# Regrouping the rows of a two-filter FFT mix, moving half a fold and most product sums to TensorE, and ordering the work by a list scheduler

## The chip, the cores and the metric

The kernel runs on one core of one Trainium2 chip. The metric is the device time of one execution in microseconds (us). The profiled span, from the first to the last instruction, is 1.5 to 2.1 us shorter than the timed run. Runs that the measurement marks as slow (over 1.5% above the fastest of the same kernel) are left out of the ratios and their intervals; the medians are over all runs, slow ones too.

## The reference, cut to what matters

```python
x = A_x                                                  # 1 x 2048 x 1024, bf16
g = sigmoid((x * gate_w).sum(-1, keepdims=True))         # one gate per row
def filt(x, w_r, w_i):                                   # weights 2048 x 513
    X = rfft2(x.astype(float32), axes=(-2, -1))
    return irfft2(X * (w_r + 1j * w_i), s=(2048, 1024), axes=(-2, -1)).astype(bfloat16)
return g * filt(x, A_w_r, A_w_i) + (1 - g) * filt(x, B_w_r, B_w_i)
```

Both filters use the same x, so the forward transform is done once. The kernel does all transforms as matmuls with constant matrices.

## The kernel before

Rows are split as n = 16 n1 + n2. *Stage 1* transforms over n1 (after "folding" each row: sums and differences of mirrored halves). *Stage d* transforms over the columns. The *forward n2 stage* finishes the row transform. Then each filter gets four products and two sums (*prod*), the *inverse n2 stage* (i1), the inverse column stage (dinv), and one last stage that mixes the two filters by the gate (s1inv). The row transform has 513 columns; the last one, column 512, is carried separately by small matmuls and small products. Every stage ends in a copy of 128x1024 from PSUM (PS in the profile, the memory that the matmuls write) to SBUF (the memory of R, RING and the other tiles that the matmuls read), called an eviction below, by ScalarE (ACT) or VectorE (DVE).

```python
# ... fold: two levels, four VectorE operations
dve(ns, tt(Sx, lo, hi, ALU.add), reads, [skey + ("S",)])
dve(ns, tt(Tx, lo, hi, ALU.subtract), reads, [skey + ("T",)])
for i, op in enumerate((ALU.add, ALU.subtract)):
    dve(ns, tt(o, f, r, op), ...)                        # second level
# ... stage 1: 8 matmuls of N=128 for each of 16 n2
# ... gate_row(c): 8 matmuls, then a one-partition copy; four of them, the last ones right before stage d

def stage_s2(kg):                                        # forward n2 stage, 128x128 weights
    fns = [mm(pslot(s, 0, [[1, 512]]), A, Q(0, 0, 512), True, False),
           mm(pslot(s, 512, [[1, 512]]), Cc, Q(0, 0, 512), True, False),
           mm(pslot(s, 1, [[1, 511]]), Cn, Q(1, 1, 511), False, True),
           mm(misc(6, kg, [[1, 1]]), Cn, Q(1, 0, 1), True, True),
           # ... two more

def prod(b, m):                                          # per filter and pair of groups
    dve(1230, tt(..., x, w, ALU.mult), r, ["t0"])
    dve(1230, tt(..., x, ws, ALU.mult), r, ["t1"])
    for c, op in enumerate((ALU.subtract, ALU.add)):     # the product sums
        dve(680, tt(..., op), [f"t{c}"], [("P", m % 2, c)])

for t in range(16 + 5):                                  # the order: loops written by hand
    if t < 16: stage_d(t)
    if 1 <= t < 17: stage_s2(t - 1)
    if t >= 5: stage_i1(0, t - 5)
    if t >= 2 and t % 2 == 0: prod(t // 18, t // 2 - 1 - t // 18 * 8)
    # ...
```

In these kernels each engine works through its own instructions in the order in which they were emitted, and semaphores hold it where data or a buffer is missing (in the first hand order below VectorE stands 4.8 us behind one eviction with eight folds to do). So the order of emission is the schedule.

Of the kernel before, what the change touches and what calls it, by code (L numbers as in the profile page):

```python
# [11 lines left out]
PW = 128  # L12
# [7 lines left out]

def make_consts():
# [4 lines left out]
    n1 = np.arange(128)[:, None, None]  # L26
    n2 = np.arange(16)[None, :, None]
    kord = (np.arange(16)[:, None] + 16 * np.arange(4)[None, :]).reshape(-1)
    k1 = kord[None, None, :]
    a = pi2 * ((16 * n1 * k1 + n2 * k1) % 2048) / 2048.0  # L30
    F = np.zeros((128, 16, 64, 2))
    F[..., 0] = np.cos(a)
    F[..., 1] = -np.sin(a)
    F[:, :, 0, 1] = (-1.0) ** np.arange(128)[:, None]
    C["F"] = F.reshape(128, 2048)
    R = np.zeros((64, 2, 16, 128))
    at = a.transpose(2, 1, 0)
    R[:, 0] = np.cos(at) / 2048
    R[:, 1] = np.sin(at) / 2048
    R[0, 1] = ((-1.0) ** np.arange(128))[None, :] / 2048  # L40
    C["RM"] = R.reshape(128, 2048)

    m = np.arange(256)[None, :]
    DM = np.zeros((128, 4, 2, 256))
    for h in range(2):
        d = (h * 128 + np.arange(128))[:, None] + 0.5
        lev, lod = 2 * m, 2 * m + 1
        les = np.where(m == 0, 512, 2 * m)
        DM[:, 0, h] = np.cos(pi2 * lev * d / 1024)
        DM[:, 1, h] = -np.sin(pi2 * lod * d / 1024)  # L50
        DM[:, 2, h] = -np.sin(pi2 * les * d / 1024)
        DM[:, 3, h] = np.cos(pi2 * lod * d / 1024)
# [11 lines left out]

    S2 = np.zeros((2, 3, 128, 128))
    KI = np.zeros((2, 2, 128, 2, 16, 4, 2))
    for z in range(2):
        for pm in range(2):
            for k2 in range(16):
                for ii in range(4):  # L70
                    i = ii if pm == 0 else 3 - ii
                    po = k2 * 8 + pm * 4 + ii
                    spec = (z == 1 and i == 0)
                    for q2 in range(16):
                        w = np.exp(-1j * pi2 * q2 * (k2 + (1 if (pm == 1 and not spec) else 0)) / 16)
                        if spec and pm == 1:
                            w = w * np.exp(-1j * pi2 * q2 * 64 / 2048)
                        r0, r1 = q2 * 8 + i * 2, q2 * 8 + i * 2 + 1
                        wr, wi = w.real, w.imag
                        if spec:  # L80
                            r = r0 if pm == 0 else r1
                            S2[z, 0, r, po] = wr
                            S2[z, 1, r, po] = wi
                        else:
                            sg = 1.0 if pm == 0 else -1.0
                            S2[z, 0, r0, po] = wr
                            S2[z, 0, r1, po] = -sg * wi
                            S2[z, 1, r0, po] = wi
                            S2[z, 1, r1, po] = sg * wr
                        cr, ci = wr, -wi  # L90
                        K = KI[z, :, po, :, q2, i, :]
                        if spec:
                            ri = pm
                            K[0, 0, ri], K[1, 0, ri] = cr, -ci
                            K[0, 1, ri], K[1, 1, ri] = ci, cr
                        else:
                            K[0, 0, 0], K[1, 0, 0] = cr, -ci
                            K[0, 0, 1], K[1, 0, 1] = -sg * ci, -sg * cr
                            K[0, 1, 0], K[1, 1, 0] = ci, cr
                            K[0, 1, 1], K[1, 1, 1] = sg * cr, -sg * ci  # L100
        S2[z, 2] = -S2[z, 1]
    C["S2"] = S2.transpose(2, 0, 1, 3).reshape(128, 768)
    C["KI"] = KI.reshape(2, 2, 128, 256).transpose(2, 0, 1, 3).reshape(128, 1024)
    gs = np.full((64, 2), 8.0)
    gs[:, 1] = -8.0
    gs[0] = 4.0
    C["GS"] = np.repeat(gs.reshape(128, 1), 16, axis=1)
    one = np.zeros((128, 2))
    one[0] = 1.0
    C["ONE"] = one  # L110
    idt = np.zeros((128, 16))
    idt[:16] = np.eye(16)
    C["ID"] = idt
# [3 lines left out]
class Op:  # L117
    __slots__ = ("eng", "idx", "fns", "deps", "raw", "dma", "clock", "need", "count", "waits", "pos")

    def __init__(self, eng, idx, fns, dma, pos):  # L120
        self.eng, self.idx, self.fns, self.dma, self.pos = eng, idx, fns, dma, pos
        self.deps, self.raw = set(), set()
        self.need = False
        self.count = 0


class Sched:
# [9 lines left out]
    def op(self, eng, fns, reads=(), writes=(), dma=False):  # L137
        if not isinstance(fns, (list, tuple)):
            fns = [fns]
# [3 lines left out]
        for k in reads:  # L143
            assert k in self.writer, k
            o.deps |= self.writer[k]
            o.raw |= self.writer[k]
        for k in writes:
            o.deps |= self.writer.get(k, set())
            o.deps |= self.readers.get(k, set())
# [84 lines left out]

def bass_gated_mix__spectral_gfnet__spectral_gfnet__prompt_kernel(
    nc, A_x, A_w_r, A_w_i, B_x, B_w_r, B_w_i, gate_w, out
):
    C = make_consts()
# [16 lines left out]
    FM = sb("FM", 2048)  # L255
    DM = sb("DM", 2048)
    S2 = sb("S2", 768)
    KI = sb("KI", 1024)
    DI = sb("DI", 2048)
    RM = sb("RM", 2048)  # L260
    GS = sb("GS", 16)
    ONE = sb("ONE", 2)
    ID = sb("ID", 16)
    V6 = sb("V6", 256)
    RING = sb("RING", 11264)
    GROW = sb("GROW", 512)
# [3 lines left out]
    ZG = sb("ZG", 16)  # L270
    G8 = sb("G8", 8)
# [8 lines left out]
    WR = {0: R5, 1: R2}  # L280


    load = {"act": 0.0, "dve": 0.0}
    slot_n = [0]
    nslots = [3]

    def slot():
        s = slot_n[0] % nslots[0]
        slot_n[0] += 1
        return s  # L290

    def dve(ns, fns, reads, writes):
        load["dve"] += ns
        return S.op("dve", fns, reads, writes)

    def ev(n, outap, inap, reads, writes, eng=None, bias=0.0):
        ca, cd = 170 + 0.833 * n, 150 + 1.04 * n
        if eng is None:
            eng = "act" if load["act"] + ca <= load["dve"] + cd + bias else "dve"
        load[eng] += ca if eng == "act" else cd  # L300
        if eng == "act":
            S.op("act", lambda e: e.activation(outap, inap, ACT.Copy), reads, writes)  # L302
        else:
            S.op("dve", lambda e: e.tensor_copy(outap, inap), reads, writes)  # L304

    def pslot(s, off, dims, p0=0, np_=128):
        return ap(PS, s * 1024 + off, dims, p0, np_)

    def misc(b, off, dims, np_=128):
        return ap(PS, b * 512 + off, dims, 0, np_)  # L310
# [7 lines left out]
    def dma(eng, pairs, reads, writes, kind=True):  # L318
        S.op(eng, [lambda e, d=d, s=s: e.dma_start(d, s) for d, s in pairs], reads, writes, dma=kind)  # L319

    def cload(eng, t, key, n):
        dma(eng, [(ap(t, 0, [[1, n]]).bitcast(dt.uint16), cst[key].ap())], [], [key])


    def xload(a, b):
        dma("sp", [(ap(R1, a * 1024, [[1024, b - a], [1, 1024]]), xv[:, a:b, :])], [], [("x", i) for i in range(a, b)])

    xload(0, 2)
    cload("sp", FM, "F", 2048)
    dma("act", [(ap(R2, 2048, [[1, 1024]], 0, 1), gate_w.rearrange("(o d) -> o d", o=1))], [], ["gw"])  # L330
    cload("act", ONE, "ONE", 2)
    for a, b in ((2, 4), (4, 8), (8, 12), (12, 16)):
        xload(a, b)
    cload("sp", DM, "DM", 2048)
    cload("sp", S2, "S2", 768)
    cload("sp", KI, "KI", 1024)
    cload("sp", GS, "GS", 16)
    cload("sp", ID, "ID", 16)

    def wload(b):  # L340

        prs = []
        T = WR[b]
        P = pit[id(T)]
        for ii in range(4):
            for c in range(2):
                for pm in range(2):
                    src = wsrc[b][c]
                    n = src.shape[-1]

                    def part(r0, step, k0, k1):
                        prs.append((AP(T, (4 * pm + ii) * P + (2 * k0 + c) * NS, [[8 * P, 16], [2 * NS, k1 - k0], [1, n]]),
                                    AP(src.tensor, src.offset + r0 * n, [[128 * n, 16], [step * n, k1 - k0], [1, n]])))
                    if pm == 0:
                        part(16 * ii, 1, 0, 16)
                    elif ii < 3:
                        part(80 + 16 * ii, -1, 0, 16)
                    else:
                        part(127, -1, 1, 16)
                        part(64, 1, 0, 1)  # L360
        dma("sp", prs, [], [("W", b)] + (["zrow", "gwt"] if b else []))
    wload(0)


    def fold(n, src, soff, tmp, st, dst, doff, p0, np_, ns, reads, skey, writes):
# [280 lines left out]
```

## Time and profile before

| | before |
|---|---|
| time, median of 2 runs | 158.36 us |
| profiled span | 155.9 us |
| busy TensorE / VectorE / ScalarE | 124.6 / 120.4 / 121.6 us |
| stage 1 ends (first matmul with DM, that of stage d) | 34.2 us |

The first lines come from the page of the kernel before: part 1 (busy time and share of the span) and part 4 (the chain of waits that ended last, by engine). PE is TensorE's matmuls, PEld its weight loads, POOL GpSimd, SPq the queue of SyncE that issues transfers; "issue" is time for which the profile shows no wait.

```profile
PE 124.6 (80%) x1015; PEld 89.8 (58%) x1024; DVE 120.4 (77%) x193; ACT 121.6 (78%) x132; POOL 0.2 (0%) x4
...
ACT 39%; PE 27%; DVE 21%; issue 6%; DMA 4%; SPq 1%; DVEq 0%
```

No engine is over 80% busy, and the chain changes hands among three engines. What is missing is found at the borders of stages. The next lines are from the timeline of the kernel before, 26 to 36 us. The columns are start, length, engine, line, operation, output <- inputs, shape and count; in brackets stands how long the engine was idle before and who ended that.

```profile
26.29 1.29 DVE L316 TENSOR_TENSOR R<-RING 128x1024 bf16<-128x1024 bf16 x2
...
28.63 1.89 PE L313 MATMUL PS<-R,G 128*1 128x512 bf16 x8
30.56 0.59 ACT L302 ACTIVATE R<-PS 1x512 bf16<-1x512 f32 x1 [0.33 <-PE PS L313]
31.20 1.89 PE L313 MATMUL PS<-R,G 128*1 128x512 bf16 x8 [0.68 <-ACT R L302]
33.12 0.59 ACT L302 ACTIVATE R<-PS 1x512 bf16<-1x512 f32 x1 [1.98 <-PE PS L313]
33.76 0.55 PE L313 MATMUL PS<-ONE,R 1*128 1x1 bf16 x16 [0.68 <-ACT R L302]
34.24 1.92 PE L313 MATMUL PS<-DM,R 128*128 128x256 bf16 x16
34.35 0.17 DVE L316 TENSOR_TENSOR ZG<-PS,GS 128x16 bf16<-128x16 f32 x1 [6.77 <-PE PS L313]
```

VectorE's folds end at 27.6 us. Then TensorE and ScalarE do the last two gate rows by turns, one partition at a time, while VectorE is idle for 6.77 us; only then does stage d start. The groups of VectorE by shape, part of the same profile, hold the operations that the change moves (busy us, mean ns | idle before):

```profile
L316 DVE TENSOR_TENSOR RING<-R 128x2048 bf16<-128x2048 bf16 x32 | 37.7, 1219 | 8.4 <-ACT R L302 8.4
L316 DVE TENSOR_TENSOR RING<-RING 128x512 bf16<-128x512 bf16 x64 | 24.0, 421 | 2.2 <-ACT RING L302 1.4
L316 DVE TENSOR_TENSOR RING<-RING 128x1024 bf16<-128x1024 bf16 x32 | 20.6, 684 | 0.3 <-PE PS L313 0.3
L316 DVE TENSOR_TENSOR R<-RING 128x1024 bf16<-128x1024 bf16 x16 | 10.3, 688 | 0.3
L316 DVE TENSOR_TENSOR RING<-R 128x1024 bf16<-128x1024 bf16 x16 | 10.3, 684 | 5.7 <-DMA R<-in_A_x_dram 5.7
```

From the top: 32 products, 64 final butterflies, 32 product sums, and the two levels of the fold. Their sum is 102.9 us.

### The profile page before, as it was taken

The page shows a single profiled execution, that of the slowest core. Times are in us where ns is not written, and L with a number is a line of the kernel's source. Part 1 is how long each engine was busy: PE and PEld are TensorE (multiplying, and loading weights), DVE is VectorE, ACT ScalarE, POOL GpSimd, SP SyncE. Part 2 cuts the span into 40 slices and gives each one's busy share as a digit, 9 for nine tenths or more (in the row PEclk, how much of TensorE's full clock was granted, in tenths as well). Part 3 has the DMA queues.
Part 4 walks back from the last instruction along what each step waited for, and adds up shares of the span by engine and source line. Part 5 has one row for each costly group of instructions (what it writes and reads, how often), then busy time and mean ns, then how long its engine had stood idle before and what let it go on. Part 6 is the DMA issues. An engine that isn't in the chain of part 4 may idle for free.

```text
span 155.9 us, 2541 instructions
## 1 busy us (share of the span) xinstructions
PE 124.6 (80%) x1015; PEld 89.8 (58%) x1024; DVE 120.4 (77%) x193; ACT 121.6 (78%) x132; POOL 0.2 (0%) x4
## 2 busy tenths in 40 slices
PE   0155887788989999999836999969999899898920
PEld 0144654345656777776524888857777666565600
DVE  0689999000489988998999999979725688999992
ACT  3045789819999899799954799999997699888850
POOL 0000000000000000000000000000000000000000
PEclk9999999999999999999985799999999999999995
DMA  4899999999999960000000000000000033343333
GB/s 148 307 427 421 293 208 212 219 233 242 252 249 254 247 199 0 0 0 4 0 0 0 1 4 0 0 0 4 0 0 1 4 135 135 128 147 135 135 135 135
DMA packets 13165, 19.53 MB, mean 125 GB/s; under 512 B 1505, under 2 KB 9825, under 8 KB 12770
## 3 DMA queue, kind: packets, MB, share of 16 engines
q1 hardware_dynamic: 13008, 19.37, 45.1%
q8 instruction: 8, 0.13, 0.4%
q10 hardware_dynamic: 146, 0.00, 0.1%
q14 instruction: 3, 0.02, 0.0%
HBM read 15.17 MB, written 4.19 MB: 124 GB/s over the span
## 4 chain that ended last, share of the span: by engine, by line
ACT 39%; PE 27%; DVE 21%; issue 6%; DMA 4%; SPq 1%; DVEq 0%
PE PS L313 27%; ACT R L302 22%; ACT RING L302 14%; DVE RING L316 11%; DVE R L316 6%; DMA R<-in_A_x_dram 4%; DVE RING L304 3%; ACT GROW L564 1%; ACT L564 1%; ACT V L302 1%; SPq L319 1%; DVEq L213 0%
## 5 line engine op out<-in xcount | busy, mean ns | idle before, releaser
L302 ACT ACTIVATE R<-PS 128x1024 bf16<-128x1024 f32 (+1 forms) x80 | 75.8, 1034 | 17.8 <-PE PS L313 17.8
L316 DVE TENSOR_TENSOR RING<-R 128x2048 bf16<-128x2048 bf16 (+1 forms) x48 | 48.0, 1040 | 14.1 <-ACT R L302 8.4
L302 ACT ACTIVATE RING<-PS 128x1024 bf16<-128x1024 f32 x40 | 42.9, 1138 | 8.0 <-PE PS L313 6.8
L316 DVE TENSOR_TENSOR RING<-RING 128x512 bf16<-128x512 bf16 (+1 forms) x96 | 44.6, 509 | 2.5 <-ACT RING L302 1.4
L313 PE MATMUL PS<-KI,RING 128*128 128x256 bf16 x256 | 33.8, 280 | 4.3 <-DVE RING L316 2.2
L313 PE MATMUL PS<-DI,R 128*128 128x256 bf16 x256 | 32.7, 273 | 1.5 <-DVE RING L304 1.2
L313 PEld LDWEIGHTS PS<-KI,RING 128*128 128x128 bf16 x256 | 24.2, 100 | 10.6 <-ACT R L302 2.8
L313 PEld LDWEIGHTS PS<-DI,R 128*128 128x128 bf16 x256 | 24.4, 98 | 8.4 <-DVE RING L304 2.2
L313 PE MATMUL PS<-FM,R 128*128 128x128 bf16 x128 | 11.8, 265 | 13.1 <-DVE R L316 13.1
L313 PEld LDWEIGHTS PS<-FM,R 128*128 128x128 bf16 x128 | 10.1, 121 | 15.0 <-DVE R L316 14.5
L313 PE MATMUL PS<-RING,S 128*128 128x1 bf16 (+2 forms) x91 | 15.8, 304 | 1.3 <-ACT RING L302 1.1
L313 PE MATMUL PS<-DM,R 128*128 128x256 bf16 x128 | 16.5, 273 | 0.3 <-ACT RING L302 0.2
L313 PEld LDWEIGHTS PS<-DM,R 128*128 128x128 bf16 x128 | 11.8, 97 | 3.0 <-ACT RING L302 1.1
L313 PEld LDWEIGHTS PS<-RING,S 128*128 128x128 bf16 x96 | 7.8, 97 | 7.6 <-ACT RING L302 1.4
L304 DVE CAST RING<-PS 128x1024 bf16<-128x1024 f32 x8 | 10.0, 1252 | 1.7 <-PE PS L313 1.7
L316 DVE TENSOR_TENSOR R<-RING 128x1024 bf16<-128x1024 bf16 x16 | 10.3, 688 | 0.3
L313 PE MATMUL PS<-R,FM 128*128 128x512 bf16 x30 | 9.1, 379 | 1.3 <-DVE RING L304 1.3
L313 PE MATMUL PS<-RING,DM 128*128 128x512 bf16 x30 | 9.1, 379 | 0.1
L313 PE MATMUL PS<-R,G 128*1 128x512 bf16 x32 | 7.5, 378 | 0.7 <-ACT R L302 0.7
L304 DVE CAST R<-PS 128x1024 bf16<-128x1024 f32 x4 | 4.9, 1224 | 3.0 <-PE PS L313 3.0
L316 DVE TENSOR_TENSOR ZG<-PS,GS 128x16 bf16<-128x16 f32 x1 | 0.2, 174 | 6.8 <-PE PS L313 6.8
L313 PEld LDWEIGHTS PS<-RING,DM 128*128 128x128 bf16 x32 | 3.1, 98 | 3.8
(25 smaller groups left out, 27.1 us busy)
## 6 DMA issues: line engine op xcount, KB each, us to landing
out_dram<-RING SPq DMA_DIRECT2D x16, 256.0 KB, 2.0
R<-in_A_x_dram SPq DMA_DIRECT2D x3, 1024.0 KB, 10.7
R<-in_A_w_r_dram SPq DMA_DIRECT2D x7, 256.5 KB, 11.5
R<-in_A_w_i_dram SPq DMA_DIRECT2D x7, 256.5 KB, 11.1
R<-in_B_w_r_dram SPq DMA_DIRECT2D x7, 256.5 KB, 6.7
R<-in_B_w_i_dram SPq DMA_DIRECT2D x7, 256.5 KB, 7.4
R<-in_A_x_dram SPq DMA_DIRECT2D x2, 512.0 KB, 5.2
FM<-c_F SPq DMA_DIRECT2D x1, 512.0 KB, 5.0
```

Source lines behind the costliest of these rows:

```text
L302: S.op("act", lambda e: e.activation(outap, inap, ACT.Copy), reads, writes)
L304: S.op("dve", lambda e: e.tensor_copy(outap, inap), reads, writes)
L313: return lambda e: e.matmul(o, l, r, start=start, stop=stop, skip_group_check=True)
L316: return lambda e: e.tensor_tensor(out=o, in0=a, in1=b, op=op)
L319: S.op(eng, [lambda e, d=d, s=s: e.dma_start(d, s) for d, s in pairs], reads, writes, dma=kind)
L564: S.op("act", lambda e: e.activation(ap(GROW, 0, [[1, 512]]), misc(7, 0, [[1, 512]]), ACT.Sigmoid), ["m7"], ["GROW"])
```

## The change

The intent: group the row frequencies by residues +-k mod 64, so that the n2 stages split into blocks of 64 that run as 64-wide tiles of the TensorE array; give the second fold level and 9 of 16 product sums to TensorE as accumulating matmuls; do the final butterflies for two rows at once; take the gate off the border between stages; and let a list scheduler, run when the program is built, choose the order, the buffers and the engine of each eviction from a small cost model. The diff replaces nearly the whole kernel; here is its core.

```diff
+DUE = {"d": (-8.69, 18.96), "s2": (-58.51, 12.61), "pa": (220.69, -19.92), ...}   # priorities, one line per stage
+SUMS = {(0, 1): 1, (0, 3): 1, (0, 4): 1, (0, 5): 1, (1, 0): 1, (1, 1): 1, (1, 4): 1}   # sums left on VectorE
+ACT_FIRST = 0.308
 ...
+def plan(tasks, pools, due, act_first, window):        # list scheduler: simulated times, engines, buffers
 ...
+        t.bytes = nbytes / rate / 1e3                  # a load's time on the wire; weights: rate 240
 ...
 # stage 1: second fold level as accumulation, [F, F] and [F, -F]
+    fns.append(mm(d, ap(RING, o + h * 128, [[1, 128]]), ff, True, False))
+    fns.append(mm(d, ap(RING, o + 256 + h * 128, [[1, 128]]), fn, False, True))
 ...
 # forward n2 stage: 64x64 tiles, r = rows of the array, a = columns
+    w = ap(SK, z + mi * 64, [[1, 64]], 64 * r, 64)
+    fns.append(mm(ps(sl, r * 512, [[1, 512]], 64 * a, 64), w, ap(RING, o, [[1, 512]], 64 * r, 64), True, False))
 ...
 # inverse n2 stage: 64-row tiles; without SUMS four terms accumulate, with SUMS two
+    comps = [(0, 0, 0), (1, 0, 2)] if summed else [(0, 0, 0), (0, 512, 1), (1, 0, 2), (1, 512, 2)]
+    fns.append(mm(ps(sl, a * 512 + lb * 128, [[1, 128]]), w, ap(SK, 384 + z + k * 128, [[1, 128]], 64 * a, 64), ...))
 ...
-    for t in range(16 + 5):
-        if t < 16:
-            stage_d(t)
 ...
+    for t in sorted(tasks, key=lambda t: (t.start, t.id)):
+        t.emit(t.eng)
```

## The prediction

> **What bounds it now.** No engine does. In the page's totals TensorE, VectorE and ScalarE are each busy 124.6, 120.4 and 121.6 us of a 155.9 us span, so some 35 us of each is waiting, and most of that lies at the borders of stages. The chain of waits is spread over ScalarE 39%, TensorE 27%, VectorE 21%. By the timeline, stage 1 ends at 34.2 us: VectorE's folds pace it until 27.6 us, then TensorE and ScalarE walk the gate row by turns for 6.6 us while VectorE idles 6.8 us; VectorE then waits 6.4 us for the first spectrum. Between 77 and 90 us the small column-512 chain adds holes, and the granted clock falls to 0.66 in the stretch 80 to 90 us. The end adds about 6 us after the last matmul.
>
> **Costs, from spacing in the timeline.** Matmul: 55 ns at N=128, 109 at N=256, 216 at N=512. PSUM eviction of 1024: 0.92 us on ScalarE (1.21 for the strided one after stage d), about 1.15 on VectorE. SBUF operation on VectorE: 0.34 us at 512, 0.60 at 1024, 1.14 at 2048.
>
> **What changes.** VectorE besides evictions: one fold level of two goes to TensorE, -10 us; 9 of 16 product sums become accumulating matmuls, -11; merged final butterflies -2.5. That leaves about 80 us. The 128 large evictions stay and are shared freely: estimate 105 us of work on each of ScalarE and VectorE, from about 119.
> TensorE: stage 1 doubles from 7 to 14 us. The forward n2 stage, as 64x64 tiles, falls from 16 x 0.99 to 16 x 0.46 us (-8). The inverse n2 stage needs 32 half-row matmuls of N=128; if pairs overlap fully that is about 0.9 us, as before, and half with VectorE sums (-4). Gate row -5. Sum: 118 to about 108 us. [...]
> So work alone buys little; order buys most.
>
> **Critical path.** Stage 1 ends near 22 us instead of 34.2, limited by x landing (about 14 us), then folds and 14 us of TensorE; the gate leaves the path. After it TensorE has about 92 us[...], ScalarE and VectorE 90 each. TensorE becomes the tightest engine and the scheduler fills the holes. 22 + 99 + 3 of bubbles + 5 tail = 129 us of span; the timed run is about 2 us longer.
>
> Prediction: 131 us, range 122 to 142. Faster by over 2%: 0.97; within 2%: 0.02; slower: 0.01.
>
> **What would show it.** First stage-d matmul near 22 us; VectorE SBUF operations down by some 24 us in the groups; TensorE over 85% busy from 25 us to the end, no hole of 2 us or more between stages; the 64x64 matmuls starting four together with 8 in about 0.46 us; 32 half-row matmuls in about 0.96 us; casts on VectorE up from 12 to about 20.
>
> **What would make it wrong.** Half-row matmuls that don't overlap: [...]the plan needs 30 ns per matmul with its weight load. At 55 ns stage i costs 1.76 us, adding up to 18 us and ending above 140. Weight loads that no longer hide in 64-column tiles. [...] W loads landing late (8.4 MB at about 240 GB/s: 35 us after x). On the good side, fewer mode changes and a better packed order would reach 123.

One of them was a term of the sum: about 7 us, the author's estimate for some 50 changes between tile shapes ("mode changes") at 0.15 us each, the part of a matmul's 272 ns beyond its 109 ns spacing in the trace before. The sum holds it: 99 is 92 plus these 7, and 22 + 99 + 3 + 5 came to 129 us of span.

## The result, and the profile after

| | before | after |
|---|---|---|
| time, median of 2 runs | 158.36 us | 137.85 us (137.08 and 138.62) |
| profiled span | 155.9 us | 136.8 us |
| busy TensorE / VectorE / ScalarE | 124.6 / 120.4 / 121.6 us | 116.4 / 97.2 / 113.4 us |
| first matmul of stage d | 34.2 us | 23.3 us |
| TensorE instructions (matmuls and weight loads) | 2039 | 3366 |

The ratio is 0.8705, with a 95% interval from 0.849 to 0.892. Ratios here and below are the mean time of one kernel's fast runs over that of the other's of the same rounds, so they are not quite the ratios of the medians. The lines of the page after (part 1, part 4) that answer to those before:

```profile
PE 116.4 (85%) x1683; PEld 86.6 (63%) x1683; DVE 97.2 (71%) x134; ACT 113.4 (83%) x123; POOL 5.3 (4%) x13
...
SPq 33%; PE 25%; DVE 24%; DMA 10%; issue 2%; ACT 2%; DVEq 0%
```

The chain now begins with the queue that issues the loads (SPq, 33%) and a transfer of B's weights (DMA, 10%). The groups of VectorE after:

```profile
L432 DVE TENSOR_TENSOR RING<-R 128x2048 bf16<-128x2048 bf16 x32 | 37.8, 1226 | 0.6 <-ACT R L436 0.6
L432 DVE TENSOR_TENSOR R<-R 128x1024 bf16<-128x1024 bf16 x32 | 20.2, 687 | 8.9 <-ACT R L436 8.7
...
L432 DVE TENSOR_TENSOR RING<-RING 128x1024 bf16<-128x1024 bf16 x14 | 9.0, 679 | 0.0
L432 DVE TENSOR_TENSOR RING<-R 128x1024 bf16<-128x1024 bf16 x12 | 7.5, 687 | 1.1 <-DMA R<-in_A_x_dram 1.1
...
L432 DVE TENSOR_TENSOR RING<-R 128x512 bf16<-128x512 bf16 x8 | 2.9, 420 | 5.7 <-DMA R<-in_A_x_dram 5.7
```

These sum to 77.4 us, 25.5 less than before. So the removed VectorE work is as foreseen. Where the span is longer than foreseen is seen in the stretches after stage 1 (start:end, length, then the busy time of PE, PEld, DVE, ACT and POOL, the granted clock, the DMA share and GB/s):

```profile
23.30:60.00 36.70, 32.60 (x524) 22.05 (x525) 27.88 (x38) 31.29 (x34) 4.54 (x8) 1.00 1.14 191
60.00:75.00 15.00, 10.30 (x345) 9.24 (x341) 12.65 (x17) 9.19 (x10) 0.00 (x0) 0.89 0.19 59
75.00:100.00 25.00, 24.54 (x492) 21.59 (x487) 21.14 (x23) 24.71 (x28) 0.00 (x0) 1.00 0.01 3
100.00:130.00 30.00, 29.69 (x207) 19.51 (x204) 21.39 (x33) 29.47 (x32) 0.00 (x0) 1.00 0.27 106
```

From 75 us on TensorE and ScalarE are both full (24.5 and 24.7 us of 25 to 100 us, then 29.7 and 29.5 of 30). The holes of TensorE, almost 9 us, lie between 23 and 75 us. The timeline of TensorE and VectorE shows them:

```profile
37.40 0.40 PE L429 MATMUL PS<-RING,SK 64*64 64x512 bf16 x2
39.08 0.62 PE L429 MATMUL PS<-RING,SK 64*64 64x512 bf16 x6 [1.28 <-issue]
...
48.57 0.62 PE L429 MATMUL PS<-SK,RING 64*128 64x128 bf16 x16 [1.63 <-DVE R L437]
...
57.78 0.26 PE L429 MATMUL PS<-QC,SK 64*64 64x7 bf16 x10 [0.49 <-issue]
...
62.35 0.35 DVE L432 TENSOR_TENSOR P<-X,R 128x32 bf16<-128x32 bf16 x2 [3.50 <-DMA R<-in_B_w_i_dram]
...
63.05 0.54 PE L429 MATMUL PS<-P,SK 64*16 64x1 bf16 x24 [2.77 <-DVE P L432]
```

There are two kinds. Near 60 us VectorE stands 3.5 us at the small product of filter B, because the last of B's weights land at 62.3 us; the scheduler's model had them landing at 52.6 us. TensorE then stands for 2.8 us. The other kind is odd: at 37.4 us TensorE stops in the middle of a group of eight matmuls that need nothing new, and the profile gives "issue". The stop before 48.57 us bears the name of a VectorE cast, but by the timeline that cast ended at 47.9 us, so something else came last.

The trace also lists DMA packets and, for each engine, every instruction, so the stops can be laid beside the packets of 16,384 bytes on the queue that the page calls "instruction" (q8). I counted TensorE's instructions in the trace (matmuls, weight loads and 34 that the trace calls EVENT_SEMAPHORE and DRAIN); three of the stops come 256 instructions apart, and each ends 1.3 to 1.7 us after a fetch packet has arrived.

```
kernel after: TensorE instructions before the stop, resume time, fetch packet (start + length), next fetch after crossing that border
 705   39.1 us   35.7 + 1.8 us   45.8 (6.7 us later)
 961   48.6 us   45.8 + 1.4 us   54.8 (6.2 us later)
1217   57.8 us   54.8 + 1.3 us   62.2 (4.4 us later)
```

So one such packet appears to hold 256 of TensorE's instructions (an estimate from the 256 instructions between two stops). The packet counts agree with it: 13 for 3366 matmuls and loads; 8 for the 2039 of the kernel before. 256 such instructions are called a block below, and the place between two blocks a border. At the four borders that TensorE crosses between 31.6 and 57.8 us, while weights stream in, the next fetch starts 4.1 to 6.7 us after the border is crossed (at the first border, at 17.2 us, 2.4 us after it); at the eight borders after the last weights have landed it starts at most 1.3 us after it. A fast stage of TensorE uses up 256 instructions about as quickly: 32 half-row matmuls with their 32 weight loads took 0.9 us, which makes 3.6 us for 256 (an estimate).

So the **theory** to test: the missing time is the weights' doing twice over, by landing late and by holding up TensorE's instruction blocks. The **rival**: the three engines are nearly full in any case, ScalarE above all, and without these stops the time would be lost elsewhere. A second question was in the prediction itself: is it the moved work or the order that buys the gain?

### The profile page after: what moved, and what is told of

Read it like the earlier page. It is cut to its first block, busy times and chain, and to the rows that moved or that the text cites. A ratio compares the mean times of both kernels' runs of the same rounds, so it can differ in the third digit from the quotient of the medians.

```text
span 136.8 us, 3788 instructions
## 1 busy us (share of the span) xinstructions
PE 116.4 (85%) x1683; PEld 86.6 (63%) x1683; DVE 97.2 (71%) x134; ACT 113.4 (83%) x123; POOL 5.3 (4%) x13
## 4 chain that ended last, share of the span: by engine, by line
SPq 33%; PE 25%; DVE 24%; DMA 10%; issue 2%; ACT 2%; DVEq 0%
SPq L452 33%; PE PS L429 25%; DVE RING L432 19%; DMA R<-in_B_w_i_dram 10%; ACT R L436 2%; DVE R L437 2%; DVE R L432 1%; DVE V L437 1%; DVE FM L432 1%; DVEq L233 0%; DVE P L432 0%; DVE ZG L432 0%
## 5 line engine op out<-in xcount | busy, mean ns | idle before, releaser
L436 ACT ACTIVATE R<-PS 128x1024 bf16<-128x1024 f32 x102 | 96.1, 1067 | 11.4 <-PE PS L429 10.8
L432 DVE TENSOR_TENSOR RING<-R 128x2048 bf16<-128x2048 bf16 (+2 forms) x52 | 48.1, 977 | 7.4 <-DMA R<-in_A_x_dram 6.8
L429 PE MATMUL PS<-DM,R 128*128 128x256 bf16 x384 | 45.2, 273 | 1.2 <-ACT R L436 1.1
L429 PEld LDWEIGHTS PS<-DM,R 128*128 128x128 bf16 x384 | 36.6, 98 | 9.5 <-ACT R L436 1.8
L429 PE MATMUL PS<-SK,RING 64*128 64x128 bf16 x800 | 26.7, 222 | 4.0 <-DVE R L437 2.1
L429 PEld LDWEIGHTS PS<-SK,RING 64*128 64x128 bf16 x800 | 23.6, 97 | 8.5 <-DVE RING L432 3.8
L432 DVE TENSOR_TENSOR R<-R 128x1024 bf16<-128x1024 bf16 x32 | 20.2, 687 | 8.9 <-ACT R L436 8.7
L429 PE MATMUL PS<-FM,RING 128*128 128x256 bf16 x128 | 15.6, 289 | 1.7 <-ACT FM L523 1.7
L429 PEld LDWEIGHTS PS<-FM,RING 128*128 128x128 bf16 x128 | 13.2, 104 | 4.7 <-ACT FM L523 2.6
L436 ACT ACTIVATE RING<-PS 128x1024 bf16<-128x1024 f32 x13 | 12.6, 1053 | 1.8 <-PE PS L429 1.8
```

Source lines behind the costliest of these rows:

```text
L429: return lambda e: e.matmul(o, l, r, start=start, stop=stop, skip_group_check=True)
L432: return lambda e: e.tensor_tensor(out=o, in0=a, in1=b, op=op)
L436: return lambda e: e.activation(o, i, ACT.Copy)
```

## The experiments

All kernels but one give the reference's result. Each ran in three rounds beside the kernel before, on three chips; the kernel before had medians of 158.87, 158.38 and 158.26 us there, so compare runs by their ratios.

| run | median us | ratio to before | 95% interval |
|---|---|---|---|
| changed kernel again | 136.69 | 0.8623 | 0.8525 to 0.8721 |
| B weights as contiguous runs (wrong result) | 133.58 | 0.8463 | 0.8396 to 0.8531 |
| at most four weight transfers queued | 138.84 | 0.8777 | 0.8702 to 0.8851 |
| true weight rate in the model | 136.58 | 0.8648 | 0.8577 to 0.8719 |
| both remedies | 133.46 | 0.8429 | 0.8395 to 0.8462 |
| new arithmetic, first hand order | 158.60 | 1.0021 | 0.9973 to 1.0069 |
| new arithmetic, second hand order | 150.56 | 0.9507 | 0.9455 to 0.9558 |
| both fold levels on VectorE | 145.71 | 0.9219 | 0.918 to 0.9259 |
| the same, priorities searched anew | 137.06 | 0.8647 | 0.8604 to 0.8689 |
| all product sums on VectorE | 146.73 | 0.9279 | 0.9222 to 0.9337 |
| the same, priorities searched anew | 136.92 | 0.8657 | 0.8618 to 0.8696 |
| all product sums on TensorE | 146.47 | 0.9188 | 0.9123 to 0.9253 |

### The changed kernel again

No edit. It gives the scatter and shows whether the stops are systematic.

> The changed kernel itself, for the scatter of the others: 137 to 139 us. Every theory expects the same here: TensorE stops for about 4 us in all near 37, 47 and 57 us, and VectorE waits about 3.5 us for the last B weight near 60 us, if these stops are systematic and not an accident of one profile.

Measured: 136.69 us, just under the expected range. TensorE again stopped at the instruction counts 705 (1.8 us beyond the usual spacing), 961 (0.6) and 1217 (0.5). B's weights landed earlier this time, and the wait for them was shorter: TensorE lost 0.9 us there instead of 2.9. So the stops stay where they are, and their lengths vary from run to run. The 1.2 us between this median and the first one are of the size of that variation.

### B's weights as contiguous runs (wrong result on purpose)

```diff
+        if b:
+            for c in range(2):
+                prs.append((ap(T_, t0 * 2 * n + c * 8 * n, [[1, 8 * n]]),
+                            AP(src.tensor, src.offset + t0 * n, [[16 * n, 128], [1, 8 * n]])))
```

> Wrong result on purpose: the B weights are read as long contiguous runs (8 KB a row piece instead of 1026 B), so they land some 10 us earlier and their packets are few; the order of all other work is unchanged. Theory 1 (the weight transfers cost the missing time, by landing late and by delaying TensorE's instruction blocks): the 3.5 us wait of VectorE and at least two of the three TensorE stops vanish, 137.9 falls to 131 to 133.5 us. Theory 2 (TensorE, ScalarE and VectorE are full behind the stalls, so slack elsewhere absorbs them): below 1.5 us gained.

Measured: 133.58 us. VectorE does not wait for a weight at all, and the stop at 961 is gone. At 1217 TensorE still stands 1.0 us, but there the block had landed 5.9 us before and the profile names a small copy by GpSimd. The stop at 705 (1.4 us) stays; A's weights still stream in at that time (until 38.1 us). This is what the theory said, just above the upper edge of its range, and more than the 1.5 us that the rival allows. Some 3 us of the changed kernel are the cost of B's weights arriving as they do.

### At most four weight transfers queued

```diff
+            ops.append(S.op("sp", [...], [("wp", k - OUTST)] if k >= OUTST else [], [("wp", k)], dma=True))   # OUTST = 4
```

> Correct result, same order of work; every weight transfer is only issued when the fourth one before it has landed, so that at most 1 MB is queued. If the blocks of TensorE's instructions come late because they queue behind the weight packets: the delay from crossing a block border to the start of its fetch (4.1, 6.7, 6.2 us now) falls below 3 us, the three TensorE stops (about 4 us) vanish, and the time falls by 1.5 to 4 us, unless pacing makes the weights land later. If the fetch is late for another reason, the delays stay and the time stays at 137 to 139 or rises with later weights.

Measured: 138.84 us, no gain. The edit did what it should: counted as above, the fetches now start 1.2 to 2.3 us after the border is crossed, and there are no more stops at 705 and 961. So the delay depends on how many loads are queued (4.1 to 6.7 us without this limit); by what mechanism, no run shows. (At 1217 TensorE again stands 1.0 us for GpSimd's copy, so the end of that stop bought nothing.) But TensorE only came sooner to the other wait. Matched matmul by matmul with the changed kernel, it gained 1.6 us at border 705 and 1.7 us at 961, and lost 3.0 us again at the wait for B's weights. These two lines are from the table of waits of this run (who waited for whom: us in total, times, longest):

```profile
DVE P L432 <- DMA R<-in_B_w_i_dram: 6.5, 1, 6.5
PE PS L429 <- DVE P L432: 5.7, 1, 5.7
```

VectorE's wait for B's weights grew from 3.5 to 6.5 us. The weights land when they land (62 us), and the order has everything wait for them. A gain of one kind turned into a wait of the other.

### The true weight rate in the scheduler's model

```diff
-        return load(f"w{b}.{t0}", prs, ..., (t1 - t0) * 262656, 240.0)
+        return load(f"w{b}.{t0}", prs, ..., (t1 - t0) * 262656, 190.0)
```

> Correct result; one number of the scheduler's model changed: the weights' rate 240 to 190 bytes per ns, as the trace shows it. The list order puts products of A before the small product that waits for the last B weight. Theory 1 (the wait of 3.5 us is on the critical path): 2 to 3.5 us less, 134 to 136 us, and no wait of VectorE for a transfer over 1 us near 60 us; TensorE's stops at instruction borders stay. Theory 2: no change, within 1 us.

Measured: 136.58 us, the same as the changed kernel of the same call; the expected 2 us did not come. The wait for weights is gone: the scheduler now puts products of filter A ahead of the small product. But a stop of the other kind got longer in its place. From the timeline of TensorE in this run:

```profile
61.67 0.25 PE L429 MATMUL PS<-GS,SCR 128*32 128x1 bf16 x13 [0.61 <-DVE V L437]
64.26 0.52 PE L429 MATMUL PS<-GS,SCR 128*32 128x1 bf16 x51 [2.34 <-issue]
```

Here the block border at 1473 instructions is reached at 61.8 us. Its fetch started at 61.7 us, 4.6 us after the border before. In the changed kernel TensorE stood for the weights at that time and reached this border only at 65.9 us, when the block had long come.

### Both remedies

The two edits above together; the order of work is that of the run before.

> Correct result: both remedies at once, at most four weight transfers of 256 KB outstanding and the true weight rate in the scheduler's model (the order is that of the run with the rate alone). If TensorE's stops at instruction borders and VectorE's wait for the last B weight are two separate losses on the critical path, each hidden behind the other when only one is mended: 131 to 133.5 us, no stop of TensorE over 1 us that the profile gives no wait for, no wait over 1 us for a weight. If something behind them holds (ScalarE's evictions, VectorE's B products): 135 to 137 us.

Measured: 133.46 us, against 136.58 and 138.84 us with one remedy each. The profile shows no wait for a weight, and the largest stop of its matmuls put down to "issue" is 0.7 us. From the page, part 1:

```profile
PE 114.9 (87%) x1683; PEld 85.3 (65%) x1683; DVE 96.9 (74%) x134; ACT 113.0 (86%) x123; POOL 7.0 (5%) x13
```

And the stretches, with columns as above:

```profile
23.50:60.00 36.50, 34.21 (x597) 23.46 (x600) 30.73 (x42) 33.61 (x36) 6.22 (x8) 1.00 0.95 196
60.00:75.00 15.00, 12.36 (x427) 11.35 (x420) 15.00 (x20) 11.66 (x14) 0.00 (x0) 1.00 0.18 62
```

At 75 us TensorE has started 1024 matmuls since stage 1, where the changed kernel had 869. The two losses were both on the critical path, and each hid behind the other, so neither remedy alone showed a gain. This version beats both kernels: its interval (0.8395 to 0.8462) lies below that of the changed kernel (0.8525 to 0.8721).

A rival that I did not name is the granted clock: from 60 to 75 us it is 0.89 in the changed kernel and 1.00 here. The changed kernel's trace has it at one half from 64.3 to 67.7 us, and 48 half-row matmuls that start at 64.1 us take 2.62 us; here 48 of the same shape take 1.51 us. So about 1 us of that profile goes with the clock. It does not explain the gain: the changed kernel's run with a mean clock of 0.992 took 137.08 us, where this kernel took 133.27 us at 0.993 and 133.65 us at 0.956.

The rival is not wholly wrong. From 75 us on, TensorE and ScalarE are full in both versions (here 24.7 and 24.9 us of the 25 to 100 us), so nothing of this kind is left to gain there.

### The new arithmetic in a first hand-written order

The list scheduler is replaced by a fixed rank for each task, a software pipeline like that of the kernel before, with evictions shared by a running balance.

```diff
+    return {"d": 2 * i, "s2": 2 * i + 2.1, "pa": 2 * i + 2.3, "ia": i + 6.2, "pb": 2 * i + 18.3, "ib": i + 22.2,
+            "da": i + 25.1, "db": i + 41.1, "o": 2 * i + 42.2, "v": 17.5 + i, "g": 12.5 + i if i < 5 else 24 + 3 * i}[k]
...
+        t.eng = min(t.cost, key=lambda e: load[e] + t.cost[e][0])
```

> The new arithmetic (regrouped rows, 64-wide tiles, half the fold and the same product sums on TensorE) in a hand-written software pipeline by stages like that of the kernel before, evictions shared by a running balance; the list scheduler is out. If order buys most of the gain, as the prediction said: 146 to 154 us. If the moved work buys most: 136 to 142 us.

Measured: 158.60 us, no faster than the kernel before. It was worse than either theory had it, and partly by faults of my order: evictions of stage 1 given to VectorE held up the folds behind them. Its timeline shows this:

```profile
13.82 2.49 DVE L397 TENSOR_TENSOR RING<-R 128x1024 bf16<-128x1024 bf16 x4
21.10 1.23 DVE L402 CAST R<-PS 128x1024 bf16<-128x1024 f32 x1 [4.79 <-PE PS L394]
22.24 4.90 DVE L397 TENSOR_TENSOR RING<-R 128x1024 bf16<-128x1024 bf16 x8
```

At 16 us VectorE had eight folds to do and stood 4.8 us behind an eviction of a result that TensorE had not made yet.

### The new arithmetic in a second hand-written order

```diff
-"v": 17.5 + i, "g": 12.5 + i if i < 5 else 24 + 3 * i
+"v": (17.5, 18.5, 26)[i], "g": 12.5 + i if i < 5 else 20 + 2 * i
+        if t.name == "d0":
+            load["act"] = load["dve"] = 0.0
-        t.eng = min(t.cost, key=lambda e: load[e] + t.cost[e][0])
+        t.eng = "act" if t.name[:3] == "evz" else min(t.cost, key=lambda e: load[e] + t.cost[e][0])
```

> A fairer hand-written order for the new arithmetic: stage-1 evictions all on ScalarE so that they don't hold up the folds, the small product that waits for the last B weight moved behind four B products, the mixing rows earlier. If the first static order lost only by these three faults: 137 to 141 us, so arithmetic alone would give nearly all of the gain. If order as such is what turns the moved work into time: 146 to 153 us.

Measured: 150.56 us, in the range of "order as such". Stage d starts at 24.0 us, as with the scheduler (23.3), so the gain of the first third needs no scheduler. The arithmetic and the moved gate do not bring it by themselves, though: with both, the first hand order started stage d at 34.0 us. The loss comes later. One example from its timeline:

```profile
65.06 1.07 PE L396 MATMUL PS<-SK,RING 64*128 64x128 bf16 x32
71.43 0.56 PE L396 MATMUL PS<-P,SK 64*16 64x1 bf16 x24 [5.30 <-DVE P L399]
```

TensorE stands 5.3 us for the small product of filter A. By the chain of waits, 3.5 us of that pass while VectorE does two products and two sums of filter B, which stand ahead of it in the queue. In the changed kernel TensorE did not wait for this product. Taken at its word, this run says that 4.9 of the 13.8 percentage points of gain come with the arithmetic in a hand order and 8.8 more with the scheduler's order. This is a bound and not a property of the work: a better hand order may exist, and the old arithmetic was never given to the scheduler.

### Both fold levels on VectorE

The second level goes back to VectorE, and stage 1 has matmuls of N=128 again.

```diff
+                        S.op(g, [tt(ap(R4, ...), ap(RING, so, [[512, nn], [1, 256]]), ap(RING, so + 256, ...), ...)], ...)
-                            fns.append(mm(d, ap(RING, o + h * 128, [[1, 128]]), ff, True, False))
-                            fns.append(mm(d, ap(RING, o + 256 + h * 128, [[1, 128]]), fn, False, True))
+                                fns.append(mm(ps(sl, k * 512 + h * 256 + hv * 128, [[1, 128]]), ap(R4, ...), ff, True, True))
```

> Undoes one part: both fold levels on VectorE, stage 1 with matmuls of N=128 again (7 us of TensorE instead of 14), all else and the list scheduler as in the change. Theory (VectorE paced stage 1): VectorE's 22 us of folds with evictions around them end stage 1 some 3 to 6 us later than 23.3 us, total 140 to 143 us. Rival (after the gate is off the path stage 1 is set by x landing and TensorE): within 1.5 us of the changed kernel.

Measured: 145.71 us, 9 us worse than the changed kernel, more than any theory had said. Stage d starts at about 27 us. But its table of waits also has a line that has nothing to do with the fold:

```profile
PE PS L429 <- DMA GW<-in_gate_w_dram: 4.1, 1, 4.1
```

The scheduler, with its optimistic weight rate, had put the gate early, and TensorE stood 4.1 us for the gate weights. The run mixes the price of the fold with the misfit of priorities that were tuned for another set of tasks. It can't be used alone.

### Both fold levels on VectorE, priorities searched anew

The same, with the true weight rate and with the numbers of DUE, ACT_FIRST and WINDOW searched at random for this set of tasks (the scheduler's own model was the judge; its times are not used here).

> Both fold levels on VectorE again, but with the scheduler's priorities searched anew for this set of tasks and the true weight rate (the first such run also waited 4.2 us for the gate row, a fault of the old priorities). If half the fold on TensorE is worth what the late end of stage 1 shows: 139.5 to 142.5 us. If the first run's loss of 9 us was mostly the misfit of the priorities: 136 to 138 us.

Measured: 137.06 us, as fast as the changed kernel and as the true-rate run (ratios 0.8647, 0.8623 and 0.8648). Stage d now starts at 26.9 us instead of 23.3, and still the end is not later: 3.6 us lost in stage 1 were won back after it, although the work after stage 1 is that of the changed kernel. Why exactly is not settled. One candidate is that the last of B's weights land near 60 us (62.3 us in the changed kernel), which would make a later start of stage d cheap; no run tests that.

### All product sums on VectorE, twice, and all on TensorE

```diff
-SUMS = {(0, 1): 1, (0, 3): 1, (0, 4): 1, (0, 5): 1, (1, 0): 1, (1, 1): 1, (1, 4): 1}
+SUMS = {(b, j): 1 for b in range(2) for j in range(8)}      # third run: SUMS = {}
```

> Undoes one part: all 16 product sums on VectorE (11 us more there by 18 x 0.60 us), half-row matmuls of TensorE halved for all (8 us less there by 18 x 0.44). Theory (all engines near full, VectorE is the tightest from 62 to 94 us): 3 to 7 us longer, 140 to 144 us. Rival (VectorE has 36 us idle in all, so it absorbs them, and TensorE gains): 134 to 137.5 us.

> All product sums on VectorE again, with the priorities searched anew and the true weight rate (the first such run waited 5.3 us for the gate row). If moving 9 of 16 sums is worth some VectorE time between 60 and 95 us: 139.5 to 142.5 us. If the first run's loss of 10 us was mostly misfit: 135.5 to 138 us.

> The other end: no product sum on VectorE, all on TensorE (VectorE 8.4 us less, TensorE 14 x 0.44 = 6 us more, and 448 more instructions than now, that is nearly two blocks of 256 more counting weight loads 3.5). Theory (TensorE is the tightest overall): 4 to 8 us longer, 141 to 146 us. Rival (VectorE between 62 and 94 us is what counts): faster than the changed kernel by 1 to 4 us.

Measured: 146.73 us with the old priorities (longer than either theory said; TensorE waited 5.1 us for the gate weights, like above, and its clock was at one half for 17 us between 39 and 77 us, whose cost is not separated), 136.92 us with priorities searched anew; all sums on TensorE, with the old priorities, 146.47 us (two of its four runs were slow; the fast ones took 144.79 and 145.78). The last one was not searched anew, so it tells no more than that priorities don't carry over. For the sums on VectorE the answer is clear: with an order fitted to it, it is as fast as the change (0.8657 beside 0.8648 for the true-rate run). It also has fewer TensorE instructions (1395 matmuls instead of 1683). So moving either part to TensorE, taken alone, was worth less than one per cent. Three things limit this: the changed kernel itself was not run with priorities searched anew, neither undone kernel was run with at most four weight transfers queued, and whether both parts can go back to VectorE together was not tried.

## Why the prediction was right or wrong

The prediction was right in what it forecast: faster, 131 us with a range of 122 to 142, and 137.85 us measured. Point by point:

- **Nothing bounds it but the borders of stages, and work alone buys little.** Supported, not shown: the second hand order keeps the new arithmetic and gains 4.9% of the time before, the scheduler's order 13.8%, but order alone, on the old arithmetic, was never run. The two undoing runs with searched priorities show that each of two moves changes the time by less than 1% once the order fits.
- **Stage 1 ends near 22 us.** It ended at 23.3 us. That is 10.9 of the 19.1 us by which the span shrank.
- **VectorE's SBUF work falls by some 24 us.** 25.5 us, from the groups.
- **64x64 tiles: 8 matmuls in 0.46 us; 32 half-row matmuls in 0.96 us.** Right: eight more in a row add 0.43 us (16 took 1.06 us, 8 took 0.63), and 32 half-row matmuls add 0.89 us (64 took 1.96 us, 32 took 1.07). The matmuls of different tiles do overlap: four 64x64 matmuls start within 10 ns (at 40.61 us), the half-row matmuls start in pairs 3 to 4 ns apart (at 33.8 us), a pair every 55 ns, and 64 one-column matmuls in 32-wide tiles start 7.6 ns apart on average (66.65 to 67.13 us, at half clock).
- **Mode changes: about 50 of 0.15 us, 7 us.** The size was off in the good direction: the order has 34, and a change after a 64x64 group cost about 0.12 us (next start after 0.55 us instead of 0.43), which makes 4 us if all 34 cost as much (an estimate).
- **105 us of work on each of ScalarE and VectorE, some 20 casts on VectorE.** Wrong in the split: ScalarE 113.4, VectorE 97.2 us busy, 13 large casts. The scheduler charges VectorE a handicap (ACT_FIRST), which the prediction does not cost. The first hand order, without it, had 105.9 and 109.7 us; no run changed the handicap alone.
- **"3 of bubbles" in "22 + 99 + 3 of bubbles + 5 tail".** This is the term of the sum that was mis-sized. From the first matmul of stage d to the last matmul, 102 us were foreseen and 106.7 measured (23.3 to 130.0 us). The usual spacing of matmuls with the mode changes explains all but about 12 us of it (an estimate from the trace): about 4 us at instruction blocks, 2.9 us at B's weights, about 4 us waiting for VectorE, mostly in its wake, and about 1 us at half clock. So the waits were some 9 us more than foreseen and the work some 4 us less (95 instead of 99); that the sum is nearer than its terms is luck. The pair of remedies gave 3.2 us of this back.
- **"5 tail".** 6.8 us, from the last matmul to the end of the span.
- **"W loads landing late" as a risk.** It came true, at 45 us (15.5 to 60.9 us) for 8.4 MB of packets instead of 35, and it had a second effect that I had not thought of, on TensorE's instruction blocks. Why the packets are slower than before (92 ns for each of 1026 bytes on average instead of 78) is open; with at most four transfers queued they took 82 and 75 ns, and the last still ended at 60.9 and 60.7 us.
- **"No hole of 2 us or more between stages."** Wrong: 2.77 us at 60.3 us. "Over 85% busy from 25 us" was just right (95.5 of 111.8 us).

## What to carry to other kernels

When a profile has two waits close behind one another, remove them together before judging either: each alone may show nothing. A schedule made by a model can rest on a wrong transfer rate (here B's weights at 52.6 us in the model, 62.3 us in the trace), so compare its landing times with the trace. And undo one part of a scheduled kernel only together with a new fit of the schedule; else what you measure is the misfit. Count the instructions of a stage that is cut into 64-row tiles, too: here 800 half-row matmuls, each with a weight load, stand for 256 (512 with all product sums on VectorE), and TensorE stopped 0.5 to 1.9 us at each of three block borders while weights streamed in.
